# A fused attention and mixture-of-experts kernel: four more experts in the 20-product first layer, its weights built earlier, and the last expert reordered

## The chip, the cores and the metric

One core of a Trainium2 chip runs the whole program. The metric is the time of one execution on the device, in microseconds, as the median of the runs shown. The profile is of one further execution, and all rows below are from it. TensorE is called PE here, VectorE DVE, ScalarE ACT, GpSimd POOL; SP is the queue that issues nearly all DMAs.

## The reference, cut to what matters

Attention with a cluster mask makes x, and a mixture of eight experts is laid over it. B=4 batches, H=8 heads, S=768 rows, D=64, so x is 3072 x 512; each expert has w1 (512 x 1024) and w2 (1024 x 512).

```
scores = scale * q @ k.T                 # per head, 768 x 768
mask   = q_assign[:, None] == k_assign[None, :]
attn   = softmax(where(mask, scores, -1e9)) @ v
x      = attn.transpose(0, 2, 1, 3).reshape(3072, 512)
P      = exp(x @ w_gate - max), normalised 8 times by rows and by columns
for e in range(8):
    h    = maximum(x @ w1[e], 0)
    out += P[:, e:e+1] * (h @ w2[e])
```

## The kernel before

**Numbers.** Matmuls run in fp16. A fp32 value is split into a high half (a scaled fp16 copy, made on ACT) and a low half (what is left, made on DVE from the fp32 value and the high half, both in SBUF). A product of two values takes three matmuls.

**Phases.** Attention of all heads and the first batch's x take the time to about 480 us. A `Planner` orders that phase: every task (loads, splits, exponentials, reductions, outputs) has a rank from the tables `KEYS` and `NUDGES`, and `RELUCT`, `EARLY`, `PATIENCE`, `STAY`, `HOLD` and `WAIT` say when an engine's plan prefers another task. From 480 to about 897 us the first batch runs through experts 0 to 6. Then come 25 **slots**: the first batch's last expert and, for each of the second, third and fourth batch, experts 0 to 7. The program numbers batches from 0, so `(2, 4)` is the third batch's fifth expert.

**A slot.** The loop at the end of the program runs over slots. In iteration n it gives PE layer 1 of slot n and layer 2 of slot n-1, in 28 steps: a step is 9 matmuls of layer 2 (`layer2b`, 256 columns, L2303) and a piece of layer 1. All other work of the slot is a task with a step at which it is issued (`plan_slot`, `at`), and every engine runs what it gets in the order of issue.

- Layer 1 comes in two forms. `layer1b` uses 7 products of blocks in place of 8 (a Strassen form): 168 matmuls of 384 columns in a slot (L1673). `layer1c` uses 20 products in place of 24 (x in 3 x 2 blocks, w1 in 2 x 4): 240 matmuls of 256 columns (L2405). `FINE = 3` gives the second form to the fourth batch alone. DVE adds each product out of PSUM into the blocks of h (L1687), and ACT and DVE do the like for the other form.
- Layer 2 is always the 7-product form: `ORDER2` names per product the block of w2 and the block of h. `minus` (L2120, POOL, 128x768) makes the sums T1 to T4 of blocks of h, `high` (L2125, ACT) and `low` (L2129, DVE, 128x768) split the seven blocks for each half g of the hidden units: 14 lows in a slot. `evict` (L2268, L2270, DVE) scales PSUM by the gate and adds it to the output.
- The 20-product form needs combinations of x and of w1 that the other form lacks. `next_u(b)` (L1619) makes the 16 combinations of x of batch b: six loads, a maximum of each (DVE), the maximum over all partitions (`spread_powers`: a store of 128 numbers to DRAM, then the broadcast load `all<-amx`, then a DVE reduction of it), sums on POOL, a high on ACT and a low on DVE (L1649) each, and a store to `xsu`. `reload_u` loads them back before the batch. `plan_extras` (L2203) makes six combinations of w1 per expert: `load_rows`, nine POOL sums, high, low (L2196), and a store to `w1x`. All of this is done in the third batch's slots. The 7-product form of a batch has `next_x(b)` (L1583) with its own `spread_powers`.
- In the second batch's slots the w2 of later experts is also summed (POOL, L355), split (L2150 on DVE) and stored.

**The order of `inputs`.** `next_x` and `next_u` are generators that the loop advances by one yield at chosen steps: in the second batch at `INPUTS_AT = (8, 15, 22, 25)`, in the third at `UNITS_AT`, every second step from 5 on. Between the issue of the broadcast load `all<-amx` and the DVE reduction of it lie two such yields.

**The last slot.** In the iteration after the last slot only layer 2 of the fourth batch's last expert is left: 252 matmuls, with nothing beside them. `HASTE` sets the steps of a few highs and lows there.

Of the kernel before, what the change touches and what calls it, by code (L numbers as in the profile page):

```python
# [8 lines left out]
F32 = mybir.dt.float32  # L9
# [11 lines left out]
P = 128  # L21
# [37 lines left out]
class Planner:  # L59
# [127 lines left out]
def attn_moe_kernel(  # L187
# [79 lines left out]
    def powers(src, n, ps_tile, pool, use):  # L267

        yield PE, 0.13, 0.107, 0.1
        ps = ps_tile()  # L270
        nc.tensor.transpose(out=ps[0:n, 0:P], in_=src, identity=ident)
        gm = pool.tile([2, 1], F32, name="gm2")
        nc.vector.tensor_reduce(out=gm[0:n], in_=ps[0:n, 0:P], axis=AX, op=ALU.max)
        yield DVE, 0.6
# [82 lines left out]
    with ExitStack() as actx:  # L357
# [183 lines left out]
        KEYS = dict(load=-795.83, split0=-299.177, split1=-169.764, split2=-270.294, assign=-887.386, place=56.074, chain=-795.952, ones=-1730.337, max=-22.408, rows=-380.671, exp=-3.788, values=5.696, out=11.693, batch=-2279.549, store=25.266, group=419.467, vsum=-220.72, group0=-1045.745, inputs=-487.095, first=831.128, high=772.934, low=-602.628, chain1=-1478.092, ones1=1457.856)  # L541
# [925 lines left out]
    FINE = 3  # L1467
# [151 lines left out]
    def next_u(b):  # L1619
# [11 lines left out]
        for i, t in enumerate(xt):  # L1631
            largest(am6[:, i : i + 1], t)
            yield
# [453 lines left out]
    def load_unit(q):  # L2087
        n, u = loads_[q - N1]
        b, e = slots[n]
        if b < FINE:  # L2090
            return load_wa(e * NP2 + u)
# [379 lines left out]
```

## Time and profile before

| | us |
|---|---|
| runs | 2276.38, 2274.78, 2276.26 |
| median | 2276.26 |
| profiled execution | 2274.21 |
| its span in the trace | 2272.4 |

The profiled execution is 1.8 us longer than the span of its instructions; it is 2.05 us under the median. The page gives the busy time of each engine and the chain of work that ended last. The windows view gives the same by stretch of time; cut at the first layer-2 matmul of each slot, it gives a table by slot. The timeline gives single instructions and the idle time ahead of them on their engine with what ended it.

### The profile page before, as it was taken

To read this page: it belongs to the slowest core of one execution; us is meant where nothing else is said; L and a number is where in the kernel's file an instruction comes from. 1 tells how busy PE (TensorE), PEld (TensorE's weight loads), DVE (VectorE), ACT (ScalarE), POOL (GpSimd) and SP (SyncE) were. 2 spreads that over 40 slices of the span, in tenths; PEclk is the share of its full clock that TensorE was granted. 3 is DMA by queue.
4 is the path that set the end of the run, shared out by engine and by line. 5 is a ranking of instruction groups with operands and counts; after the bars stand their busy time and mean duration, and the time that the engine had idled before them with its cause. 6 is when DMAs were issued, how large, how long until landed. Compare 5 with 4: busy or idle time off the path is not lost.

```text
span 2272.4 us, 41784 instructions
## 1 busy us (share of the span) xinstructions
PE 2240.5 (99%) x16163; PEld 1591.9 (70%) x16163; DVE 1692.1 (74%) x2700; ACT 1175.6 (52%) x2125; POOL 1364.7 (60%) x1214
## 2 busy tenths in 40 slices
PE   8999999999999999999999999999999999999998
PEld 5666666645555555777777777777777788888887
DVE  7876777868677785878888877788887765556656
ACT  5676777646766763444444434444444434443432
POOL 7787878844577871666567536577776533333343
PEclk9999999999999999999999999999999999999999
DMA  7656676366767743876666556766666665555553
GB/s 155 147 146 148 166 173 161 101 217 212 247 190 222 241 142 135 289 273 205 206 233 228 199 185 229 251 214 213 214 222 227 230 196 171 160 174 164 168 167 93
DMA packets 284079, 438.35 MB, mean 193 GB/s; under 512 B 78296, under 2 KB 203048, under 8 KB 283880
## 3 DMA queue, kind: packets, MB, share of 16 engines
q1 hardware_dynamic: 283736, 435.64, 61.5%
q8 instruction: 127, 2.08, 0.4%
q14 instruction: 72, 0.59, 0.1%
q10 hardware_dynamic: 144, 0.03, 0.0%
HBM read 312.46 MB, written 94.64 MB: 179 GB/s over the span
## 4 chain that ended last, share of the span: by engine, by line
PE 93%; DVE 3%; DMA 2%; ACT 2%; issue 1%; POOL 0%; SPq 0%; DVEq 0%; ACTq 0%; POOLq 0%
PE h_ps L1673 28%; PE pb L2303 13%; PE h_ps L2405 9%; PE pa L2303 9%; PE pc L2303 8%; PE av_ps L1191 5%; PE exp_ps L1131 3%; PE o_ps L1936 3%; PE o_ps L1937 3%; PE o_ps L1938 3%; PE max_ps L1015 3%; PE exp_ps L1132 2%; PE misc_ps L740 1%; DMA kX<-ot 1%; PE misc_ps L860 1%
## 5 line engine op out<-in xcount | busy, mean ns | idle before, releaser
L2303 PEld LDWEIGHTS <-ho 128*128 128x128 f16 x6300 | 616.9, 98 | 126.1 <-DVE ho L2129 5.5
L1673 PEld LDWEIGHTS <-wa 128*128 128x128 f16 x4032 | 394.0, 98 | 235.5 <-issue 7.0
L1673 PE MATMUL h_ps<-xsT,wa 128*128 128x384 f16 x2304 | 436.0, 326 | 1.3 <-DVE u L1687 0.8
L2129 DVE TENSOR_TENSOR ho<-h,ho 128x768 f16<-128x768 f32 x300 | 363.7, 1215 | 35.4 <-ACT ho L2125 35.2
L2303 PE MATMUL pb<-w2o,ho 128*128 128x256 f16 x2700 | 342.5, 273 | 0.4 <-DVE ho L2129 0.4
L1673 PE MATMUL h_ps<-xsB,wa 128*128 128x384 f16 x1728 | 327.6, 326 | 2.2 <-DMA w2o<-w2d 2.1
L2125 ACT CAST ho<-h 128x768 f16<-128x768 f32 x300 | 240.7, 824 | 14.6 <-PE pa L2303 6.5
L2405 PE MATMUL h_ps<-xu,wa 128*128 128x256 f16 x1920 | 246.2, 273 | 0.0
L2120 POOL TENSOR_TENSOR h<-h 128x768 f32<-128x768 f32 x50 | 92.3, 1846 | 254.3 <-DVE ho L2129 239.2
L2340 ACT ACTIVATE h<-h 128x384 f32<-128x384 f32 x204 | 106.0, 519 | 254.4 <-DVE h L1687 254.2
L1019 DVE TENSOR_REDUCE mrt<-max_ps 128x1 f32<-128x512 f32 (+1 forms) x288 | 192.0, 684 | 58.1 <-PE max_ps L1015 55.5
L2303 PE MATMUL pa<-w2o,ho 128*128 128x256 f16 x1800 | 230.2, 274 | 2.2 <-DVE ho L2129 1.7
L2303 PE MATMUL pc<-w2o,ho 128*128 128x256 f16 x1800 | 228.7, 273 | 2.4 <-DVE ho L2129 2.4
L1687 DVE SCALAR_TENSOR_TENSOR u<-h_ps,m 128x384 f32<-128x384 f32 x192 | 106.0, 552 | 136.1 <-PE h_ps L1673 131.7
L2405 PEld LDWEIGHTS <-wa 128*128 128x128 f16 x1920 | 187.9, 98 | 21.7
L1153 POOL TENSOR_TENSOR psum<-psum,pe 128x512 f32<-128x512 f32 x150 | 196.7, 1324 | 9.9 <-ACT pe L1138 8.0
L1138 ACT ACTIVATE pe<-exp_ps 128x512 f32<-128x512 f32 x288 | 167.5, 598 | 52.8 <-PE exp_ps L1132 44.5
L2120 POOL TENSOR_TENSOR h<-h,T 128x768 f32<-128x768 f32 x50 | 108.0, 2160 | 138.8 <-DVE ho L2129 136.7
L1191 PE MATMUL av_ps<-pe,vn 128*64 128x512 f32 (+1 forms) x768 | 133.5, 491 | 0.0
L1938 PE MATMUL o_ps<-wb,hl 128*128 128x512 f16 x336 | 127.3, 379 | 0.0
L1937 PE MATMUL o_ps<-wb,hh 128*128 128x512 f16 x336 | 127.3, 379 | 0.0
L1936 PE MATMUL o_ps<-wb,hh 128*128 128x512 f16 x336 | 127.3, 379 | 0.0
(339 smaller groups left out, 3880.7 us busy)
## 6 DMA issues: line engine op xcount, KB each, us to landing
w2o<-w2d SPq DMA_DIRECT2D x175, 512.0 KB
wa<-w1d SPq DMA_DIRECT2D x70, 896.0 KB
r<-in_moe_w SPq DMA_DIRECT2D x60, 512.0 KB
wa<-w1d SPq DMA_DIRECT2D x224, 128.0 KB
raw<-in_moe_w SPq DMA_DIRECT2D x52, 512.0 KB
w1d<-wa SPq DMA_DIRECT2D x26, 896.0 KB
w2d<-w2s SPq DMA_DIRECT2D x28, 512.0 KB
wa<-w1x SPq DMA_DIRECT2D x48, 256.0 KB
```

The costliest lines, as they stand in the source:

```text
L1019: nc.vector.tensor_reduce(out=t["mr"][:, i0 : i0 + ni, ni - 1], in_=ps.rearrange("p (x c) -> p x c", x=ni), axis=AX, op=ALU.max)
L1153: (nc.gpsimd if e == POOL else nc.vector).tensor_tensor(out=st[:, o : o + N0], in0=old[o], in1=part, op=ALU.add)
L1191: nc.tensor.matmul(av[o, a:z], vn[:, i, :], heads[t]["pe", c][:, i - i0], start=(i == 0), stop=False, skip_group_check=True)
L1673: nc.tensor.matmul(ps[:, 0:HB], wa[:, a, w_, c, :], x[:, x_, c, :], start=(first and s_ == 0), stop=(s_ == len(steps) - 1), skip_group_che ...
L1936: nc.tensor.matmul(po[i], hh[:, t, ti], wbh[:, t], start=(first and t == 0), stop=False)
L1937: nc.tensor.matmul(po[i], hh[:, t, ti], wbl[:, t], start=False, stop=False)
L1938: nc.tensor.matmul(po[i], hl[:, t, ti], wbh[:, t], start=False, stop=(last and t == 1))
L2120: nc.gpsimd.tensor_tensor(out=t, in0=d[a], in1=d[c], op=ALU.subtract)
L2125: nc.scalar.copy(t[:, 0], blocks[n, g][o])
L2129: nc.vector.tensor_tensor(out=t[:, 1], in0=blocks[n, g][o], in1=t[:, 0], op=ALU.subtract)
L2303: nc.tensor.matmul(ps[:, q], h[:, h_, f, q * P : (q + 1) * P], w[:, 2 * g + f, w_], start=(first and g == 0 and s_ == 0 and q % 2 == 0), s ...
L2405: nc.tensor.matmul(ps[:, f], wa[:, at_ * P : (at_ + 1) * P], units[rank + x_][:, c], start=(p in FRESH and f == 0 and s_ == 0), stop=(s_ = ...
```

## The change

Five things are altered.

1. `FINE` becomes `(2, 4)` and is compared with slots: experts 4 to 7 of the third batch use `layer1c` too. `xsu` exists for both batches.
2. The combinations of w1 are made in other tasks: `load_extra`, nine sums of 128x128, one high and one low of 128x768, and a store, for each half f of each of two row blocks c, 36 sums per expert where there were 18 of 128x256. For experts 4 to 7 this lies in the second batch's slots, two slots per expert; for experts 0 to 3 in the third batch's slots 0 to 3.
3. `next_x(2)`, `next_u(3)` and `next_u(2, known=True)` (which needs no maximum) follow each other from slot (1, 1) on, at every second step from 2 on (`UNITS_AT`), in the second batch as well. `reload_u` of the third batch lies in slot (2, 3), that of the fourth inside the last 20-product layer of the third.
4. The last slot's layer 2 takes the first three products for g=0, then for g=1. `HASTE` covers more blocks, six of the split blocks go to buffers of other pools (`SPARE`), T1 of g=1 goes to a buffer of its own, and T4 is made earlier.
5. The planner's tables are new, and in the scale chain `yield DVE` stands ahead of the reduction.

```diff
-    FINE = 3
+    FINE = (2, 4)
...
-        for i, t in enumerate(xt):
-            largest(am6[:, i : i + 1], t)
-            yield
-        am = gs.tile([P, 1], F32, name="am")
-        nc.vector.tensor_reduce(out=am, in_=am6, axis=AX, op=ALU.max)
-        yield from spread_powers(am, 1, f"amx{b}", lambda g: input_use(b, g, gs))
+        if not known:
+            am6 = gs.tile([P, 6], F32, name="am6")
+            for i, t in enumerate(xt):
+                largest(am6[:, i : i + 1], t)
+                yield
...
+    def plan_extras(e, first, times):
+        for i, t in enumerate(times):
+            c, f = divmod(i, 2)
+            at(first + t[0], load_extra, e, c, f)
+            for m in range(9):
+                at(first + t[1] + m // 3, extra_sum, e, m)
+            at(first + t[1] + 3, extra_high, e)
+            at(first + t[1] + 4, extra_low, e)
+            at(first + t[1] + 7, extra_store, e, c, f)
...
-        if b == FINE - 1:
-            plan_extras(e, base - SLOT)
+        if b == 2 and e < (FINE[1] or E):
+            plan_extras(e, base - SLOT, [(5 * i - 4, 4 + 5 * i) for i in range(4)])
+        if b == 1 and FINE[1] and e >= FINE[1]:
+            n_ = slots.index((1, 2 * (e - FINE[1])))
...
+        if n == NS - 1:
+            order[0:6] = [(i, g) for g in range(2) for i in range(3)]
...
-    UNITS_AT = tuple(range(5, 27, 2))
+    UNITS_AT = tuple(range(2, 28, 2))
+    EARLY_AT = 16
...
-            if e == 1 and b + 1 < B:
-                inputs = next_u(b + 1) if b + 1 >= FINE else next_x(b + 1)
+            if e == 1 and (b + 1, 0) < FINE:
+                inputs = next_x(b + 1)
+                if b == 1 and FINE[1]:
+                    inputs = chain(inputs, next_u(3), next_u(2, True))
...
-            if s in (UNITS_AT if n < NS and slots[n][0] == FINE - 1 else INPUTS_AT):
+            if s in (UNITS_AT if n < NS and slots[n] > (1, 0) else INPUTS_AT):
```

**DVE in slot (1, 2).** A piece of DVE's queue in the iteration that has layer 1 of the second batch's third expert (1034.06 to 1088.87 us in the trace of before). `ho` are lows for layer 2, `u` and `h` from `h_ps` the adds out of PSUM, `w2s` a low of w2, `xst` a low of x. Before:

```order
L2129 TENSOR_TENSOR ho<-T_12242,ho 128x768
L2270 SCALAR_TENSOR_TENSOR acc<-pc,gates,acc 128x256 x3
L1687 SCALAR_TENSOR_TENSOR u_12381<-h_ps,m_12359 128x384
L2129 TENSOR_TENSOR ho<-h_11538,ho 128x768
L324 TENSOR_REDUCE am_11741<-xqB_11748 128x1
L2150 SCALAR_TENSOR_TENSOR w2s<-s2w,s_92,w2s 128x4x256
L1687 SCALAR_TENSOR_TENSOR u_12430<-h_ps,m_12359 128x384
L2129 TENSOR_TENSOR ho<-h_11875,ho 128x768
L1687 SCALAR_TENSOR_TENSOR h_12187<-h_ps,u_12430 128x384
L2270 SCALAR_TENSOR_TENSOR acc<-pb,gates,acc 128x256 x3
L1687 SCALAR_TENSOR_TENSOR h_12187<-h_ps,m_12359 128x384
L2129 TENSOR_TENSOR ho<-h_11537,ho 128x768
```


The same stretch with the change:

```order
L2138 TENSOR_TENSOR ho<-T_12336,ho 128x768
L2289 SCALAR_TENSOR_TENSOR acc<-pc,gates,acc 128x256 x3
L1688 SCALAR_TENSOR_TENSOR u_12485<-h_ps,m_12463 128x384
L2138 TENSOR_TENSOR ho<-h_11573,ho 128x768
L2159 SCALAR_TENSOR_TENSOR w2s<-s2w,s_92,w2s 128x4x256
L1688 SCALAR_TENSOR_TENSOR u_12535<-h_ps,m_12463 128x384
L2138 TENSOR_TENSOR ho<-h_11920,ho 128x768
L347 SCALAR_TENSOR_TENSOR xst<-xqB_11639,sx,xst 128x768
L1688 SCALAR_TENSOR_TENSOR h_12280<-h_ps,u_12535 128x384
L2289 SCALAR_TENSOR_TENSOR acc<-pb,gates,acc 128x256 x3
L1688 SCALAR_TENSOR_TENSOR h_12280<-h_ps,m_12463 128x384
L2138 TENSOR_TENSOR ho<-h_11572,ho 128x768
```


The low of x, `xst<-xqB_11639`, has come in between two lows for layer 2 and the next add; the reduction `am` of `next_x(2)` is gone from here, and those of `next_u(3)` come at the end of the iteration. Over the whole iteration six lows `xst`, two lows `w2s` of the new weights and four reductions `am` of 512 elements stand there where one reduction of 768 and one small one stood.

**SP around the broadcast load.** DMAs in the order of issue around `all<-amx`; `wa` are weights of layer 1, `w2o` of layer 2, `r` rows for the sums. Before, in slot (2, 1), for `next_u(3)`:

```order
L2133 DMA w2o<-w2d_6261 128x2048
L1562 DMA amx_17127<-am 128x1
L2133 DMA w2o<-w2d_6262 128x2048
L1580 DMA wa<-w1d_108 128x3584
L2201 DMA w1x_6299<-w2s 128x2048
L1565 DMA all_17180<-amx_17127 128x128
L2201 DMA w1x_6299<-w2s 128x1024
L2133 DMA w2o<-w2d_6262 128x2048
```


With the change there are two such places in the second batch, the first for `next_x(2)`:

```order
L1562 DMA amx_11986<-am 128x1
L2146 DMA r_12008<-in_moe_w 128x2x512
L2164 DMA w2d_6263<-w2s 128x4x512
L1565 DMA all_12038<-amx_11986 128x128
L2142 DMA w2o<-w2d_6263 128x2048
L1580 DMA wa<-w1d_108 128x3584
L2142 DMA w2o<-w2d_6263 128x2048
```


and the second for `next_u(3)`:

```order
L1562 DMA amx_13153<-am 128x1
L1580 DMA wa<-w1d_114 128x3584
L2142 DMA w2o<-w2d_6264 128x2048
L1565 DMA all_13202<-amx_13153 128x128
L2164 DMA w2d_6265<-w2s 128x4x512
L2176 DMA r_13251<-in_moe_w 128x2x256 x2
L2142 DMA w2o<-w2d_6264 128x2048
```


Between the store `amx` and the broadcast load stand two transfers in each of the two places, where three stood in the third batch.

**DVE in the last slot.** From the gates of the last expert on; `C` and `acc` are evictions. Before:

```order
L1728 TENSOR_SCALAR gates<-pr,so 128x6
L2270 SCALAR_TENSOR_TENSOR C_21954<-pb,gates,C_21954 128x256 x3
L2129 TENSOR_TENSOR ho<-h_26027,ho 128x768
L2129 TENSOR_TENSOR ho<-h_26521,ho 128x768 x2
L2129 TENSOR_TENSOR ho<-T_26586,ho 128x768
L2129 TENSOR_TENSOR ho<-T_26668,ho 128x768
L2270 SCALAR_TENSOR_TENSOR C_21954<-pa,gates,C_21954 128x256 x3
L2270 SCALAR_TENSOR_TENSOR acc<-pa,gates,acc 128x256 x6
L2270 SCALAR_TENSOR_TENSOR acc<-pc,gates,acc 128x256 x3
L2129 TENSOR_TENSOR ho<-h_26003,ho 128x768
L2129 TENSOR_TENSOR ho<-h_26067,ho 128x768
```


With the change:

```order
L1729 TENSOR_SCALAR gates<-pr,so 128x6
L2289 SCALAR_TENSOR_TENSOR C_22566<-pb,gates,C_22566 128x256 x3
L2138 TENSOR_TENSOR ho<-h_27133,ho 128x768
L2138 TENSOR_TENSOR ho<-T_27203,ho 128x768
L2138 TENSOR_TENSOR w2s<-h_26639,w2s 128x768
L2138 TENSOR_TENSOR ho<-tx,ho 128x768
L2138 TENSOR_TENSOR ho<-T_27283,ho 128x768
L2138 TENSOR_TENSOR r_27269<-h_26679,r_27269 128x768
L2138 TENSOR_TENSOR w2s<-h_27133,w2s 128x768
L2289 SCALAR_TENSOR_TENSOR C_22566<-pa,gates,C_22566 128x256 x3
L2138 TENSOR_TENSOR s2w<-h_26679,s2w 128x768
L2289 SCALAR_TENSOR_TENSOR acc<-pa,gates,acc 128x256 x6
```


The lows up to the first eviction of `pa` are seven where they were five (with `r` and `w2s` as new places of the low halves), two more, of B21 and B22, stand ahead of the gates, and the six evictions of `acc<-pa` stand behind one low more.

## Rows read from the trace of the kernel before

**Rows 1.** The page, part 1: busy us of each engine, share of the span, instructions.
```profile
PE 2240.5 (99%) x16163; PEld 1591.9 (70%) x16163; DVE 1692.1 (74%) x2700; ACT 1175.6 (52%) x2125; POOL 1364.7 (60%) x1214
```

**Rows 2.** Windows by phase: stretch and length (us), busy us (instructions), clock, DMA share, GB/s.
```profile
0.00:480.00 480.00, 461.77 (x2847) 291.17 (x2847) 360.35 (x659) 321.28 (x741) 371.98 (x450) 0.99 0.61 146
...
925.00:1830.00 905.00, 902.85 (x6961) 680.89 (x6959) 735.69 (x1088) 401.65 (x644) 565.86 (x407) 1.00 0.66 225
```

**Rows 3.** Windows by single slot, columns as in rows 2.
```profile
924.44:979.25 54.81, 54.81 (x422) 41.10 (x421) 45.67 (x66) 24.68 (x39) 38.09 (x26) 1.00 0.81 287
...
1034.06:1088.87 54.81, 54.81 (x422) 41.09 (x421) 47.25 (x66) 24.14 (x38) 37.37 (x27) 1.00 0.60 202
...
1417.73:1474.85 57.12, 54.97 (x422) 41.09 (x421) 42.77 (x78) 23.05 (x38) 32.54 (x27) 1.00 0.75 238
...
1694.09:1748.90 54.81, 54.81 (x422) 41.09 (x421) 41.49 (x65) 23.29 (x38) 33.49 (x27) 1.00 0.65 226
...
1803.39:1857.10 53.71, 53.71 (x495) 48.14 (x493) 33.89 (x54) 19.50 (x31) 19.41 (x12) 1.00 0.61 194
...
2232.41:2272.40 39.99, 30.20 (x254) 25.00 (x251) 29.23 (x44) 11.80 (x16) 12.34 (x6) 0.94 0.35 106
```

**Rows 4.** Chain of waits in a seven-product slot: start (us), us, engine, output, line, count.
```profile
1040.09 0.98 PE pa L2303 x9
1041.08 0.98 PE h_ps L1673 x6
```

**Rows 5.** Chain of waits in a twenty-product slot.
```profile
1961.73 1.31 PE h_ps L2405 x12
```

**Rows 6.** Timeline in the 57.12 us slot: start, us, instruction, [idle before <- releaser].
```profile
1463.44 0.32 SPq L1565 DMA_DIRECT2D all<-amx  x1
...
1472.06 0.29 DVE L1569 TENSOR_REDUCE gmax<-all 128x1 f32<-128x128 f32 x1 [4.64 <-DMA all<-amx]
...
1473.28 0.55 DVE L1687 SCALAR_TENSOR_TENSOR h<-h_ps,m 128x384 f32<-128x384 f32 x1
...
1473.88 1.14 PE L1673 MATMUL h_ps<-xsB,wa 128*128 128x384 f16 x6 [2.15 <-DMA w2o<-w2d]
```

**Rows 7.** Timeline of the last expert's second layer.
```profile
2235.81 1.92 PE L2303 MATMUL pc<-w2o,ho 128*128 128x256 f16 x16 [1.05 <-DVE ho L2129]
...
2241.27 1.92 PE L2303 MATMUL pc<-w2o,ho 128*128 128x256 f16 x16 [1.36 <-DVE ho L2129]
...
2250.20 5.55 PE L2303 MATMUL pa<-w2o,ho 128*128 128x256 f16 x34 [1.67 <-DVE ho L2129]
...
2263.45 4.09 PE L2303 MATMUL pb<-w2o,ho 128*128 128x256 f16 x36
...
2267.58 1.27 DVE L2270 SCALAR_TENSOR_TENSOR C<-pb,gates,C 128x256 f32<-128x256 f32 x3 [2.66 <-PE pb L2303]
```

**Rows 8.** DVE's groups by line, 924 to 1803 us: busy us, mean ns of one.
```profile
L2129 DVE TENSOR_TENSOR ho<-h,ho 128x768 f16<-128x768 f32 x193 | 251.3, 1302 | 0.0
...
L2196 DVE SCALAR_TENSOR_TENSOR w2s<-s2w,s,w2s 128x512 f16<-128x512 f32 x16 | 13.4, 840 | 0.0
...
L347 DVE SCALAR_TENSOR_TENSOR xst<-tx,sx,xst 128x768 f16<-128x768 f32 x4 | 5.0, 1248 | 0.0
...
L324 DVE TENSOR_REDUCE am<-xqB 128x1 f32<-128x512 f32 x4 | 2.7, 675 | 0.0
```

**Rows 9.** DVE's timeline in the second batch.
```profile
980.90 2.15 DVE L2129 TENSOR_TENSOR ho<-h,ho 128x768 f16<-128x768 f32 x1
...
983.45 2.37 DVE L2150 SCALAR_TENSOR_TENSOR w2s<-s2w,s,w2s 128x1024 f16<-128x1024 f32 x1
...
992.27 0.94 DVE L2129 TENSOR_TENSOR ho<-T,ho 128x768 f16<-128x768 f32 x1
```

**Rows 10.** POOL's timeline over the same time.
```profile
984.69 2.79 POOL L2120 TENSOR_TENSOR h<-h,h 128x768 f32<-128x768 f32 x1
```

**Rows 11.** POOL's groups by line, 924 to 1803 us: busy us, mean ns of one.
```profile
L2181 POOL TENSOR_TENSOR s2w<-s2w,r 128x256 f32<-128x256 f32 x96 | 95.1, 991 | 7.3
```

More of the change, by code (lines that the diff above doesn't have):

```diff
@@ L2084, in attn_moe_kernel @@
     blocks, parts_, lefts, sums_, gates_of = {}, {}, {}, {}, {}
-    loads_ = [(n, u) for n, (b, _) in enumerate(slots) for u in range(7 if b >= FINE else NP2)]
+    loads_ = [(n, u) for n in range(NS) for u in range(7 if slots[n] >= FINE else NP2)]
     def load_unit(q):
@@ L2089, in load_unit @@
         b, e = slots[n]
-        if b < FINE:
+        if slots[n] < FINE:
             return load_wa(e * NP2 + u)
@@ new lines, in extra_sum, with part @@
+        r, x = sums_[e, "r"][0], sums_[e, "x"]
+        def part(t, m):
+            return t[:, m * P : (m + 1) * P]
+        o, _, *a = EXTRAS[i]
+        old = a[0] == "x"
+        first, sign, second = a[1:] if old else a
+        quad = [part(r, int(m) % 2 * 4 + int(m) // 2) for m in (first, second)]
+        nc.gpsimd.tensor_tensor(
+            out=part(x, int(o)), in0=part(x, int(first)) if old else quad[0], in1=quad[1], op=ALU.add if sign == "+" else ALU.subtract
+        )
+        if i == 8:
+            sums_[e, "r"] = sums_[e, "r"][1:]
@@ L2216, in plan_slot @@
+    SPARE = {(o, g): x for g in range(2) for o, x in zip(("B21", "B22", "T3"), (
+        (rp, [P, 2, 2 * DO], "r2"), (sp, [P, 4, 2 * HD], "s2w"), (w2p, [P, 8, HD], "w2s"),
+    ))}
+    HASTE = {
[3 rows of a table added]
+    }
     def plan_slot(n):
@@ L2219, in plan_slot @@
         base = SLOT * (n + 1)
-        fine = b >= FINE
-        for g, (t1, t2, t3, t4) in enumerate(((-3, -2, -1, 9), (2, 3, 4, 11) if fine else (1, 2, 3, 11))):
+        fine, last = slots[n] >= FINE, n == NS - 1
+        for g, (t1, t2, t3, t4) in enumerate(((-3, -2, -1, 5 if last else 9), (1, 2, 4, 7) if last else (2, 3, 4, 11) if fine else (1, 2, 3, 11))):
             at(base + t1, minus, n, g, "T1", "B12", "B11", "B11")
@@ L2422, in attn_moe_kernel @@
     for n in range(NS + 1):
-        one = (layer1c(n) if slots[n][0] >= FINE else layer1b(n)) if n < NS else iter(())
+        one = (layer1c(n) if slots[n] >= FINE else layer1b(n)) if n < NS else iter(())
         two = layer2b(n - 1) if n else iter(())
@@ L2442, in attn_moe_kernel @@
                 f(*a)
-            if s in (UNITS_AT if n < NS and slots[n][0] == FINE - 1 else INPUTS_AT):
+            if s in (UNITS_AT if n < NS and slots[n] > (1, 0) else INPUTS_AT):
                 step(inputs)
+            if s == EARLY_AT and n + 1 < NS and slots[n + 1] == FINE:
+                for _ in inputs:
+                    pass
+                for i in (0, 1, 6, 7):
+                    reload_u(FINE[0], i)
             step(two)
```

116 lines of the change are left out of this document (54 added, 62 removed), and 3 rows, old and new, of the table HASTE.

## The prediction

> **What bounds the kernel now.** I read the page's engines first: PE is busy in 99% of the span [rows 1], so time is won only where PE's own work shrinks or where PE stands still. The windows by phase say where it stands still: 18 us of the first 480 are not busy, 2.1 of the 905 us of the second and third batch [rows 2]. Cut by slot, a slot of the second or third batch is 54.81 us long and PE is busy for all of it, a slot of the fourth batch 53.71, one slot 57.12, and the last stretch 39.99 with 30.20 of PE [rows 3]. So the slots are bound by PE's stream of matmuls, at a granted clock of 1.00; the exceptions are one stall and the tail. DVE is the next engine: 41 to 47 us of a 54.81 us slot [rows 3].
>
> The profiled execution took 2274.21 us, 2.05 under the median of 2276.26; I add the changes to the first and then 2.05.
>
> **Four slots in 20 products.** The chain of waits shows six matmuls of 384 columns in 0.98 us, so 0.163 each, and nine of 256 columns in 0.98, so 0.109 [rows 4]; in the other form twelve of 256 columns take 1.31, again 0.109 [rows 5]. Layer 1 falls from 168 x 0.1625 = 27.30 to 240 x 0.1092 = 26.20 us, so −1.10 for a slot; whole slots say the same, 54.81 − 53.71 [rows 3]. Four slots: **−4.4**. A clock or operand reason against it isn't in the rows, as the fourth batch runs this form from end to end. Its combinations of x come by DMA: one combination is used last 6 of 20 products before the next slot wants its successor, 6 x 2.7 = 16 us, against 384 KB at the 194 GB/s of such a slot [rows 3], 2 us. That is covered, at nothing; without the cover it would be 2 us for the load that comes late.
>
> **The stall in slot (2, 1).** The row of PE that stands still names a weight load, 2.15 us [rows 6]. DVE's rows tell the cause: the broadcast load `all<-amx` is issued at 1463.44, the reduction that wants it waits 4.64 us until 1472.06, and the add that PE wants stands behind it on DVE until 1473.83 [rows 6]. The transfer took 8.6 us with a DMA share of 0.75 in that slot. With the change `next_u(3)` is no longer in this slot: **−2.3** (57.12 − 54.81). But `next_x(2)` and `next_u(3)` both make such a load in the second batch now, with the reduction two yields, that is four steps of about 2 us, behind its issue, as in the slot that stalls. (`next_x(2)` had seven steps and more between.) In SP's order two transfers stand between the store and the broadcast load, where three did. Each costs between 0, where the load lands in time, and 2.15 [rows 6], together 0 to 4.3. I take **+1.5**, nearer to the lower end: 4.64 us of waiting on DVE cost 2.15 on PE, so 2.5 are hidden by the lead that DVE has, and the slots concerned, but for their neighbours, show DMA shares of 0.60 [rows 3].
>
> **DVE in the second batch.** This is the cost. New work in these slots: sums, highs, lows and stores for the weights of four experts, 16 combinations of x for each of two batches, and the maxima. In slot (1, 2) the order adds six lows of x, at 1.248 or somewhat less, 6.6 to 7.5 us; two lows of the new weights of 128x768, with 0.84 for 128x512 [rows 8], so 1.7 to 2.7; and four reductions at 0.675 [rows 8] for one of 768, +1.6. That is +10 to +11.8 on 47.25 us [rows 3]: 57.3 to 59 us of DVE in a slot of 54.81. The other seven slots, counted in the same way, get 2 to 7 us more and reach 45 to 54. Where DVE is late, PE waits for the adds, since a PSUM bank comes free only with them; up to 2.5 us late costs nothing [rows 6].
>
> The durations themselves depend on POOL. A low of 128x768 takes 0.94 alone and 2.15 where POOL runs; the low of w2 takes 2.37, and POOL's subtraction of the same time 2.79 [rows 9, 10]; the mean of all such lows is 1.30 [rows 8], with POOL busy 566 of 905 us, a share of 0.63 [rows 2]. So sharing costs 0.36 a low. POOL gets 18 sums of 128x128 more in such a slot; a sum of 128x256 takes 0.99 [rows 11], so I estimate 0.45 each and 45 us of POOL in slot (1, 2), a share of 0.82. In proportion a low grows by 0.11, and 26 lows by about 2.5 us. At the lower end, then, slot (1, 2) is 2.5 us over and the lead hides it: 0 to 0.5. At the upper it is 4.2 + 2.5 over, and two slots at 54 grow by 2 each and are over by 1 each: 9. I take **+3.5**.
>
> The Trainium skill (SBUF — State Buffer, section "Who interferes with whom") says that a DVE instruction with two inputs in SBUF and a GpSimd instruction that reads SBUF take a shared pair of ports in turn, the first for its whole instruction while the other fully blocks. The rows above agree (0.94 against 2.15). It speaks against this change, which puts such instructions on both engines in the same slots, and is the mechanism of the second rival.
>
> **The last slot.** Its layer 2 is 252 matmuls, 252 x 0.1092 = 27.5 us, yet from 2232.41 to the end of the last matmul at 2267.54 it takes 35.13 [rows 7]. PE waits for lows at three places, 1.05, 1.36 and 1.67 us [rows 7], and between them it is fed slowly. With the change two lows are made ahead of the gates, T1 of the second half gets a buffer of its own and need not wait for a low that reads the old one, and the first 108 matmuls come in the order in which halves of h are ready. Going through the new order with the durations of these rows, I find a wait of 1.2 for T2's low and one of 2.2 for the six evictions of `pa` ahead of the next product, and the last matmul 31.5 to 33 us after the first. Nothing beyond it changes (1.27 of eviction [rows 7], then the store). **−3.0**, from −4.5 to −1.5.
>
> **The attention phase.** The new ranks reorder the first 480 us; the matmuls there are the same ones. All that can be won is the 18 us in which PE is not busy [rows 2]; a third of it, 6 us, to either side is my bound, since nothing there says which tasks are late now. I take **−1.5**: the waits are many and short, which is what other ranks can move, yet they can't all go. In the third batch the moved work takes load off, but PE never waits there but for the stall, so that is worth nothing.
>
> **Sum.** −4.4 − 2.3 + 1.5 + 3.5 − 3.0 − 1.5 = −6.2: 2274.2 → 2268.0 in the profiled execution, 2270.0 as a median.
>
> **The rivals.**
> - *Same.* Both broadcast loads stall PE as the one before did (+4.3), and DVE's lateness costs 6, with the rest as above: −11.2 + 10.3 = −0.9, about 2275. For it: the same four steps, and a second batch with DMA shares to 0.81 [rows 3]. Against it: DVE's lead. The attention phase losing 6 in place of winning 1.5 ends near there too, at −6.2 + 7.5, 2277.6.
> - *Slower.* DVE becomes the bound of the second batch. If POOL's work were beside every low, sharing would cost 0.36 / 0.63 = 0.57 a low, 0.21 more than in the mean; with the longer lows of w2 that makes about 5.7 us a slot on top of the 48 to 58 us, and six slots are over 54.81, by 23 us in all. All else is −9.7, so +13: 2289.6. It decides from 14.3 us of PE's waiting on (−9.7 + 14.3 = +4.6). For it: both engines' queues are filled at the same steps. Against it: POOL has 10 us free in the fullest slot, and the adds read PSUM.
> - *Faster still.* The ranks of the attention phase are worth 6 in place of 1.5: 2265.5.
>
> **How the numbers follow.** The forecast (2270, itself 2265 to 2275) 0.56, same 0.27, slower 0.09, faster still 0.08. A measurement of this kernel tells from no change about 0.2%, 4.6 us, so 2271.7 is the line for faster: 0.45 of the forecast's 0.56 lies under it and 0.11 over it. Faster 0.45 + 0.08 = 0.53; same 0.11 + 0.27 = 0.38; slower 0.09. The range of 2263 to 2279 leaves out the slower rival and the far end of the fastest.
>
> **What would show it.** Slots (2, 4) to (2, 7) at 53.71 (right) or longer (then the loads of combinations are late); slot (2, 1) at 54.81; slot (1, 2) and its neighbours at 54.8 to 60, with PE's idle time released by DVE's adds; one row of waiting for `all<-amx` at each of two places; the last stretch at 37 in place of 39.99; PE's busy time of the first 480 us unchanged, with the layer of the first expert starting some us earlier or later. If slots of the second batch other than (1, 2) are over 56, the term of DVE is wrong; if the last stretch is over 39, that of the tail.

## The result

The changed kernel takes 2303.6 us (median of 4 runs, 2302.66 to 2307.62) against 2276.32 before: a ratio of 1.0124, interval 1.0106 to 1.0141 (ratios here and below are those on record; that of the two medians is 1.0120). It is 27 us slower where 6 us less were forecast. The profiled execution took 2303.82 us with a span of 2302.0.

The page's first part, as rows 1 before:

```profile
PE 2244.9 (98%) x16451; PEld 1618.3 (70%) x16451; DVE 1704.1 (74%) x2685; ACT 1194.3 (52%) x2141; POOL 1453.8 (63%) x1381
```

PE's busy time is 4 us more than in [rows 1], though four slots have less to compute, and POOL has 89 us more. The windows by slot, each cut at the slot's first layer-2 matmul (stretch and length, then busy us of PE, PEld, DVE, ACT and POOL with their instructions, granted clock, DMA share, GB/s), answer to [rows 3]:

```profile
921.19:976.00 54.81, 54.81 (x422) 41.09 (x420) 48.13 (x68) 26.36 (x41) 50.26 (x44) 1.00 0.85 300
976.00:1043.21 67.21, 58.56 (x423) 42.44 (x421) 54.84 (x78) 26.73 (x41) 48.48 (x45) 0.95 0.69 233
1043.21:1107.23 64.02, 56.40 (x421) 41.01 (x420) 59.63 (x75) 30.62 (x46) 50.30 (x44) 1.00 0.82 285
1107.23:1168.50 61.27, 56.69 (x423) 41.64 (x421) 50.40 (x80) 27.44 (x43) 45.81 (x45) 0.97 0.81 232
...
1224.24:1283.46 59.22, 56.64 (x421) 41.84 (x420) 53.70 (x74) 29.07 (x46) 52.03 (x47) 0.97 0.76 259
...
1338.68:1393.49 54.81, 54.81 (x422) 41.10 (x420) 44.13 (x66) 24.02 (x40) 35.32 (x32) 1.00 0.70 232
1393.49:1450.46 56.97, 55.13 (x422) 41.08 (x420) 47.50 (x71) 26.49 (x43) 46.82 (x49) 1.00 0.79 264
1450.46:1505.82 55.36, 55.11 (x423) 41.09 (x421) 46.37 (x70) 26.41 (x43) 44.53 (x48) 1.00 0.71 233
...
1616.34:1670.05 53.71, 53.71 (x495) 48.14 (x492) 31.36 (x51) 19.49 (x32) 19.43 (x12) 1.00 0.59 181
...
2260.20:2302.00 41.80, 30.57 (x254) 25.59 (x251) 30.08 (x42) 9.39 (x13) 14.95 (x7) 0.90 0.33 101
```

The second batch's slots, 54.81 us each before, are 54.81, 67.21, 64.02, 61.27, 55.74, 59.22, 55.22 and 54.81: 33.8 us more. The first slot starts 3.3 us earlier than before. The 20-product slots are at 53.71, as forecast. The third batch's first three slots are 56.97, 55.36 and 56.03, the last stretch 41.80 in place of 39.99 (41.76 and 39.95 if it is counted from the start of its first matmul itself, as below). So −3.3 + 33.8 + 1.3 (third batch, experts 0 to 3) − 4.1 (experts 4 to 7) + 1.8 (last stretch) are 29.5, and the span is 29.6 longer.

What PE waited for, over the whole span (engine, line, releaser: us in total, times, longest):

```profile
PE h_ps L1674 <- DVE h L1688: 16.6, 13, 3.6
PE h_ps L1674 <- DVE u L1688: 10.3, 8, 4.1
...
PE pb L2324 <- DVE ho L2138: 3.5, 1, 3.5
...
PE pa L2324 <- DVE acc L2289: 2.3, 1, 2.3
```

The first two groups are the adds out of PSUM on DVE. In the second batch alone they are 16.0 and 7.9 us, and no other wait of PE is listed there. The whole second batch in one window, before and with the change:

```profile
924.44:1362.92 438.48, 438.48 (x3362) 328.77 (x3361) 363.62 (x523) 195.49 (x308) 264.97 (x180) 1.00 0.66 225
...
921.19:1393.49 472.30, 448.02 (x3362) 331.27 (x3360) 414.10 (x572) 221.79 (x344) 386.35 (x339) 0.99 0.77 255
```

So the 33.8 us have two parts: for 24.3 PE is not busy, and 9.5 are PE's own busy time, 448.0 in place of 438.5 for the same matmuls. Most of the second part (7.5) lies in the three slots with a granted clock of 0.95 to 0.97. DVE is busy for 414 of the 472 us, and the mean of its lows, here from 921 to 1616 us, has hardly moved from [rows 8]:

```profile
L2138 DVE TENSOR_TENSOR ho<-h,ho 128x768 f16<-128x768 f32 x145 | 192.4, 1327 | 0.9 <-ACT ho L2134 0.8
```

So DVE is not out of time there; it stands still. What it waits for in the second batch, besides PE:

```profile
DVE gmax L1569 <- DMA all<-amx: 9.5, 2, 5.7
DVE am L324 <- DMA xqB<-xd: 7.1, 2, 3.6
DVE w2s L2207 <- ACT w2s L2203: 7.0, 5, 2.6
```

and what ACT waits for on POOL in the second batch (before, the second of these groups had 10.0 us in 8 waits, and the first didn't exist):

```profile
ACT w2s L2203 <- POOL s2w L2190: 36.8, 12, 7.3
...
ACT w2s L2155 <- POOL s2w L355: 12.1, 10, 2.6
```

Two thirds of POOL's new sums of 128x128, from 921 to 1616 us (the others take 0.72 in the mean):

```profile
L2190 POOL TENSOR_TENSOR s2w<-s2w,r 128x128 f32<-128x128 f32 x192 | 125.3, 653 | 15.0
```

Two patterns make up these waits. The first is a read that stands too close behind its DMA. In slot (1, 1), for `next_x(2)`:

```profile
1027.83 0.33 SPq L1565 DMA_DIRECT2D all<-amx  x1
...
1031.36 1.15 PE L2324 MATMUL pb<-w2o,ho 128*128 128x256 f16 x9
...
1033.65 0.28 DVE L1569 TENSOR_REDUCE gmax<-all 128x1 f32<-128x128 f32 x1 [5.70 <-DMA all<-amx]
...
1036.04 0.55 DVE L1688 SCALAR_TENSOR_TENSOR u<-h_ps,m 128x384 f32<-128x384 f32 x1
...
1036.64 1.14 PE L1674 MATMUL h_ps<-xsT,wa 128*128 128x384 f16 x6 [4.14 <-DVE u L1688]
...
1037.62 1.95 PE L2324 MATMUL pb<-w2o,ho 128*128 128x256 f16 x9
```

The broadcast load is issued at 1027.83; its reduction waits 5.70 us at the head of DVE's queue, the add behind it ends at 1036.6, and PE has stood still for 4.14. The nine matmuls of layer 2 after the gap take 1.95 us, the nine ahead of it 1.15: PE runs at a lower granted clock there (0.80 from 1036 to 1039, 0.63 from 1039 to 1042). The second pattern is in the chain of waits at the end of slot (1, 4) (start, us, engine, output):

```profile
1218.69 0.42 POOL s2w L2190
...
1220.19 0.94 ACT w2s L2203
...
1221.16 1.58 DVE w2s L2207
...
1223.21 2.02 DVE ho L2138
1225.24 2.21 DVE xst L1650
1227.44 0.48 DVE h L1688
...
1227.97 1.17 PE h_ps L1674 x6
```

POOL's last sum of a piece of the new weights ends at 1220.2; ACT's high of it waits at the head of ACT's queue, DVE's low for the high, and behind that low stand another low, a low of x and then the add that PE needs: four engines in a row, each in order.

### The profile page after: what moved, and what is told of

The parts are those of the page before. It is cut to its first block, busy times and chain, and to the rows that moved or that the text cites. A ratio compares the mean times of both kernels' runs of the same rounds, so it can differ in the third digit from the quotient of the medians.

```text
span 2302.0 us, 42812 instructions
## 1 busy us (share of the span) xinstructions
PE 2244.9 (98%) x16451; PEld 1618.3 (70%) x16451; DVE 1704.1 (74%) x2685; ACT 1194.3 (52%) x2141; POOL 1453.8 (63%) x1381
## 4 chain that ended last, share of the span: by engine, by line
PE 76%; DVE 11%; POOL 5%; DMA 4%; issue 2%; ACT 2%; SPq 0%; DVEq 0%; POOLq 0%; ACTq 0%
PE h_ps L1674 15%; PE h_ps L2429 14%; PE pb L2324 9%; PE pc L2324 6%; PE pa L2324 6%; PE av_ps L1191 5%; PE exp_ps L1131 3%; PE max_ps L1015 3%; PE exp_ps L1132 3%; PE o_ps L1937 2%; PE o_ps L1938 2%; PE o_ps L1939 2%; DVE ho L2138 2%; POOL s2w L2190 2%; POOL s2w L355 2%
## 5 line engine op out<-in xcount | busy, mean ns | idle before, releaser
L1674 PEld LDWEIGHTS <-wa 128*128 128x128 f16 x3360 | 329.3, 98 | 236.7 <-issue 41.0
L1674 PE MATMUL h_ps<-xsT,wa 128*128 128x384 f16 x1920 | 364.2, 327 | 22.8 <-DVE h L1688 11.7
L2429 PE MATMUL h_ps<-xu,wa 128*128 128x256 f16 x2880 | 369.3, 273 | 0.0
L2429 PEld LDWEIGHTS <-wa 128*128 128x128 f16 x2880 | 281.8, 98 | 32.6
L1674 PE MATMUL h_ps<-xsB,wa 128*128 128x384 f16 x1440 | 275.8, 328 | 7.6 <-DVE h L1688 4.9
L2361 ACT ACTIVATE h<-h 128x384 f32<-128x384 f32 x156 | 81.0, 520 | 175.7 <-DVE h L1688 175.3
L1688 DVE SCALAR_TENSOR_TENSOR u<-h_ps,m 128x384 f32<-128x384 f32 x160 | 88.1, 551 | 100.1 <-PE h_ps L1674 93.7
L2406 ACT ACTIVATE h<-h_ps 128x512 f32<-128x512 f32 x108 | 64.4, 596 | 171.3 <-PE h_ps L2429 125.2
L2396 POOL TENSOR_TENSOR h<-h,tx 128x512 f32<-128x512 f32 x12 | 23.0, 1913 | 204.2 <-DVE tx L2408 204.2
L2190 POOL TENSOR_TENSOR s2w<-s2w,r 128x128 f32<-128x128 f32 x192 | 125.3, 653 | 15.0
L2408 DVE SCALAR_TENSOR_TENSOR h<-h_ps,h 128x512 f32<-128x512 f32 x96 | 65.2, 689 | 92.4 <-PE h_ps L2429 73.8
```

The source lines that it names most:

```text
L1674: nc.tensor.matmul(ps[:, 0:HB], wa[:, a, w_, c, :], x[:, x_, c, :], start=(first and s_ == 0), stop=(s_ == len(steps) - 1), skip_group_che ...
L1688: nc.vector.scalar_tensor_tensor(out=t, in0=ps[:, 0:HB], scalar=KAPPA, in1=x, op0=ALU.mult, op1=ALU.add)
L2190: nc.gpsimd.tensor_tensor(out=part(x, int(o)), in0=part(x, int(first)) if old else quad[0], in1=quad[1], op=ALU.add if sign == "+" else AL ...
L2429: nc.tensor.matmul(ps[:, f], wa[:, at_ * P : (at_ + 1) * P], units[rank + x_][:, c], start=(p in FRESH and f == 0 and s_ == 0), stop=(s_ = ...
```

## The experiments

The theories: (1) data are read too soon behind their DMA; (2) DVE has too much work, shared with POOL; (3) POOL is behind its steps, and ACT and DVE wait for it in order. The table gives by how many us the second batch's slots (1, 1) to (1, 6) exceed 54.81. The slots are those of one profiled execution each, and so is the time, but for the first row. Two runs further down (old form of the last expert, T1 in place) have the same second batch as the changed kernel, and theirs exceeds by 35.9 and 32.4 us in all where the changed kernel's does by 33.8, so 2 us more or less in such a sum are noise.

| kernel | (1,1) | (1,2) | (1,3) | (1,4) | (1,5) | (1,6) | time |
|---|---|---|---|---|---|---|---|
| changed | 12.4 | 9.2 | 6.5 | 0.9 | 4.4 | 0.4 | 2303.6 |
| later reads | 2.1 | 12.6 | 0 | 5.6 | 4.4 | 0.5 | 2298.3 |
| no four weights | 3.3 | 7.1 | 3.5 | 0.2 | 0.5 | 1.5 | 2285.7 |
| wide sums | 6.3 | 9.8 | 6.4 | 0 | 1.1 | 1.5 | 2290.5 |
| later reads, wide sums | 0 | 5.5 | 0.9 | 2.1 | 1.1 | 1.7 | 2277.6 |
| later reads, no four weights | 0 | 1.6 | 0 | 0.3 | 0.5 | 1.5 | 2273.7 |
| fourth batch only | 3.5 | 7.2 | 0 | 0 | 0 | 0 | 2297.5 |
| the same, old steps | 0 | 0 | 0 | 0 | 0 | 0 | 2280.4 |

The kernel before took 2276.2 us beside later reads, no four weights and fourth batch only, 2275.7 beside wide sums and old steps, and 2273.5 beside the two combined edits.

**Later reads** (first run).

```diff
+            for _ in range(2):      # behind the loads of x
+                yield
...
+        for _ in range(more):       # 2, behind the broadcast load
+            yield
```

> The changed kernel, but in the second batch's slots four yields more lie between a DMA and the DVE instruction that reads what it brought: two (about 8 us) between the loads of x and the first maximum, two more between the broadcast load and its reduction, for both inputs. Theory 1 (DVE, which works in order, stands still for data that was asked for too late, and PE with it): the four DVE waits of 3.5, 5.7, 3.6 and 3.8 us go, PE's gaps of 3.3, 4.1 and 3.6 us in slots (1,1) to (1,3) with them; 2303.6 falls by 9 to 14 us to about 2292. Theory 2 (DVE has simply more work than time in these slots, shared with POOL): the waits only let DVE catch up less; under 4 us are won, at least 2299.5.

2298.3: 5.3 us, between the two; the second batch is 8.5 shorter and the third 2.9 longer. DVE's waits for DMAs are gone and with them most of the excess of (1, 1) and all of that of (1, 3), but the work that moved on made (1, 2) and (1, 4) longer. There ACT waits 4.7 and 7.9 us for POOL's sums, and 5.8 and 6.6 for a store of the new weights, for which it waited 2.0 in the second batch of the changed kernel:

```profile
ACT w2s L2161 <- DMA w1x<-w2s: 14.0, 3, 6.6
```

The names suggest that the high of w2 wants a buffer `w2s` that this store still reads; no run tests that. Theory 1 is right for two slots and is not the whole.

**No weights for the four experts** (second run).

```diff
-                nc.sync.dma_start(out=o, in_=w1x[e][:, :, EXTRA.index(p)])
+                nc.sync.dma_start(out=o, in_=w1x[e % FINE[1]][:, :, EXTRA.index(p)])
...
-            plan_extras(e, SLOT * n_, [...])
```

> The changed kernel without the new weights of experts 4 to 7: their sums, highs, lows, loads and stores in the second batch's slots are left out, and the 20-product layer of these experts reads the combinations of expert e-4 (same sizes and times). Theory 2 (too much work on DVE and POOL): PE is held up by 33.8 us in the second batch; the 16 lows and 144 sums are the larger part of what is new, so 14 to 22 us are won, about 2285. Theory 1 (reads too soon behind their DMAs): the four waits stay, slots (1,1) to (1,3) stay over 58 us, and less than 8 us are won, over 2295.

2285.7, 18 us less. (1, 1) to (1, 3) still exceed by 14, as theory 1 says. The weights' work is the larger part of the loss; the run takes away its load on DVE and POOL, its lateness and its transfers together, so it doesn't tell them apart.

**The fourth batch only, and the old steps** (third and sixth run).

```diff
-    FINE = (2, 4)
+    FINE = (3, 0)
```

> The changed kernel with the 20-product first layer in the fourth batch alone: no weights and no combinations of x for it in the second batch. All else is as changed (ranks of the attention phase, last expert, weights in pieces of 128 columns). If the second batch's work is the whole loss: the second batch's slots are at 54.81 again; 2276.3 - 3.2 (attention, earlier start of the first slot) + 1.8 (last slot) gives 2273 to 2277. If the smaller pieces of the weights or their short runs in the stores cost by themselves, the third batch's slots are above 55.5 and the time is over 2280.

2297.5, far over what was expected, and not for the reason that was named: (1, 1) and (1, 2) exceed by 3.5 and 7.2 as with the four experts, since `next_x(2)` keeps its close steps; the third batch's slot (2, 1) is 62.4 (57.12 before), again at the broadcast load. The last stretch was 43.3 here. Next, the steps as before on top of it:

```diff
-    UNITS_AT = tuple(range(2, 28, 2))
+    UNITS_AT = tuple(range(5, 27, 2))
...
-            if s in (UNITS_AT if n < NS and slots[n] > (1, 0) else INPUTS_AT):
+            if s in (UNITS_AT if n < NS and slots[n][0] == 2 else INPUTS_AT):
```

> The kernel of the third run (20 products in the fourth batch alone) with the steps for the inputs as before the change: four per slot in the second batch, every second step from 5 on in the third. If the closer steps of next_x(2) alone held up slots (1,1) and (1,2) there (58.3 and 62.0 us): both are at 54.81 again, and the time falls by at least 10.6 us, to 2284 to 2287; the third batch's slots stay above 54.81 where the new weights are made in smaller pieces. If the order of the attention phase or the form of the weights did it, they stay over 57 and the time over 2292.

All eight slots of the second batch are at 54.81 again, and the time is 2280.4, under the range expected, with an earlier start and a shorter third batch than in the run above. So the close steps alone cost 10.6 us in the second batch, with none of the new work there. The third batch's slots stay at 55.6 to 58.6 (54.81 at (2, 6)), as expected with the weights in smaller pieces: that batch takes 450.4 us where it took 440.5 before.

**Wide sums** (fifth run). Three POOL sums of 256 columns in place of nine of 128:

```diff
-            for m in range(9):
-                at(first + t[1] + m // 3, extra_sum, e, m)
+            for m in range(3):
+                at(first + t[1] + m, wide_sum, e, m)
```

> The changed kernel with three POOL sums of 256 columns in place of nine of 128 for each piece of the new weights; the sums are not those that the weights need. DVE's and ACT's instructions and all DMAs stay. Theory 3 (POOL is behind its steps with the nine sums; ACT's high waits for them, in order, DVE's low waits for the high, in order, and PE for the add behind that low): ACT's waits for these sums in the second batch fall from 36.8 us to under 10, the excess of slots (1,3) to (1,6) from 12.2 us to under 4, and the time by 8 to 14 us to 2290 to 2296. Theory 2 (DVE's own load of lows and adds is too much): DVE has the same load, under 4 us are won, at least 2299.

2290.5, 13.1 us less, with DVE's instructions untouched; ACT's waits for these sums fall to 13.9 us, not under 10. That is theory 3's range, though (1, 3) stays at 6.4, held by the broadcast load. 8.8 us come from the second batch, the rest from the third and an earlier start. DVE is busy for as long as before the edit:

```profile
919.17:1382.65 463.48, 444.74 (x3362) 329.85 (x3360) 413.89 (x572) 221.96 (x344) 337.36 (x243) 0.99 0.78 261
```

So the gain doesn't come from a shorter time of DVE's work, which speaks against the reading that POOL cost these 8.8 us by slowing DVE's lows.

**Both edits, and later reads without the weights** (ninth and tenth run). The edits are those of the first with the fifth, and of the first with the second.

> The changed kernel with both earlier edits: the four yields of the first run and the three wide sums of the fifth (sums that the weights don't need). If early reads and POOL's lateness are separate causes, their gains add, 5.3 + 13.1: about 2285, with the waits of DVE for loads gone and ACT's waits for the sums under 15 us. If the two stand in for one another (what one gives up the other takes): 2289 or more.

> The changed kernel without the new weights of experts 4 to 7 (the layer reads those of expert e-4) and with the four yields. Of the 16.1 us by which the second batch's slots were too long without the weights, slots (1,1) and (1,3) gave 6.8 and slot (1,2), which has the lows of x, 7.1. If early reads explain the first and DVE's load the second: (1,1) and (1,3) near 54.81, the slot with the lows of x still 59 to 63, about 2279. If early reads explain all: 2272. If the close steps load DVE throughout: 2284.

2277.6, below both numbers expected, and 2273.7, between the first two, with the slot of the lows of x at 56.4, under its range. In the second batch the later reads save 8.5 us, the wide sums 8.8, both 22.6. That they gain more together fits a lead that each cause uses up for the other, and gaps that cost more by the clock when they are long; no run separates these two. With both, ACT's waits for the new sums are nearly gone, and DVE's work is still all there:

```profile
ACT w2s L2218 <- POOL s2w L2207: 4.6, 3, 2.2
...
918.49:1368.17 449.68, 441.19 (x3363) 328.63 (x3361) 410.79 (x568) 219.48 (x341) 336.96 (x240) 1.00 0.80 266
```

DVE is busy for 410.8 us, against 414.1 in the changed kernel and 363.6 before, and the excess is 11.2 us in place of 33.8: the amount of work on DVE is not what cost the other 22.6.

With the reads later and no weights the fullest slot is 1.6 over:

```profile
1028.43:1084.85 56.42, 55.16 (x423) 41.06 (x421) 54.89 (x78) 29.84 (x45) 39.25 (x27) 1.00 0.78 277
```

DVE is busy 54.89 of 56.42 us there, and the second batch exceeds by 3.8 in all: without the weights' work the share of theory 2 is small. What the 11.2 us with both edits are made of stays open: ACT waits 8.5 us there for stores of the new weights. A run with the highs and lows of the weights at later steps, the straight test of theory 3, was not made.

**The attention phase** (seventh run), and the stall of slot (2, 1) (eighth run, with `more` = 2 as in the first), on the kernel before:

```diff
-        KEYS = dict(load=-795.83, ...)      # and the other tables, as in the change
+        KEYS = dict(load=-362.213, ...)
```

> The kernel before with only the new ranks and planner's constants of the attention phase and the place of the yield in the scale chain. The first slot starts 3.2 us earlier, as in the changed kernel, and nothing gives it back: 2272.5 to 2273.5. If the later phases use up the lead (the first batch's slots are paced by loads): 2275 to 2277.

2269.6 against 2275.7: 0.9978, interval 0.9968 to 0.9988, so 2.7 to 7.3 us. The sign was right; the size is open, since the phase itself varies: with the same ranks the first slot started at 918.1 us in this profile and at 925.0 in the next one.

> The kernel of the run beside it with two yields (about 8 us) more between the broadcast load of next_u and its reduction. If DVE's wait for that load is the whole of the 57.12 us slot: it is 54.81 us long and the time 2.3 us less than beside it, 2270 to 2271. If another load is late there, under 1 us.

Slot (2, 1) is 54.81 in place of 57.34 us: the broadcast load was the whole of that stall. The time is 2268.9 (0.9971, 0.9962 to 0.9980), 0.6 from the run beside it, which these runs don't resolve.

**The last expert.** The old form in the changed kernel (fourth run; order, `HASTE`, `SPARE`, T1 and T4 as before the change):

> The changed kernel with the order, buffers and steps of the last expert as before. If the new order of the last expert is worse by itself (two pairs of lows beside POOL's subtractions at 2.55 us each): the stretch from its first matmul to the end falls from 41.8 to 40.0 us, and the time by about 1.8 to 2301.8. If something ahead of it made it longer, it stays at 41 to 42.

2303.0; the last stretch is 38.33 in place of 41.76 us, so the new form is worse by itself. (The same old form took 39.95 in the kernel before, where the granted clock was 0.59 and 0.56 from 2250 to 2254 us; here it stayed at 1.00.) In the changed kernel:

```profile
2266.17 2.55 DVE L2138 TENSOR_TENSOR ho<-T,ho 128x768 f16<-128x768 f32 x1
2267.87 2.52 POOL L2124 TENSOR_TENSOR h<-h,h 128x768 f32<-128x768 f32 x1
...
2268.65 2.55 DVE L2138 TENSOR_TENSOR w2s<-h,w2s 128x768 f16<-128x768 f32 x1
...
2268.78 3.60 PE L2324 MATMUL pb<-w2o,ho 128*128 128x256 f16 x16 [3.50 <-DVE ho L2138]
...
2278.69 2.43 DVE L2289 SCALAR_TENSOR_TENSOR acc<-pa,gates,acc 128x256 f32<-128x256 f32 x6
...
2281.18 4.09 PE L2324 MATMUL pa<-w2o,r 128*128 128x256 f16 x36 [2.33 <-DVE acc L2289]
```

Three lows in a row (two are shown) take 2.55 or 2.56 us each, one beside each subtraction on POOL (2.52); PE waits 3.50 for the first, then 2.33 for evictions that stand behind the lows on DVE. Four runs looked for the cause, the first in the changed kernel, the others with the new form of the last expert in the kernel of the eighth run; the edits, in their order:

```diff
# T1 in place
-        if n == NS - 1 and (o, g) == ("T1", 1):
-            t = tmp.tile([P, KC, HB], F32, name="tx")
# evictions first
-        ("T3", 0): (2, 2), ... ("B21", 1): (1, 6), ("T3", 1): (7, 7), ("B22", 1): (2, 8),
+        ("T3", 0): (2, 9), ... ("B21", 1): (1, 10), ("T3", 1): (7, 11), ("B22", 1): (2, 12),
# old order
-        if n == NS - 1:
-            order[0:6] = [(i, g) for g in range(2) for i in range(3)]
# on DVE
-        nc.gpsimd.tensor_tensor(out=t, in0=d[a], in1=d[c], op=ALU.subtract)
+        (nc.vector if n == NS - 1 else nc.gpsimd).tensor_tensor(out=t, in0=d[a], in1=d[c], op=ALU.subtract)
```

> The changed kernel with T1 of the last expert's second half in its old place, so that POOL waits there again for the low that reads the block. If the wait that was taken away had kept POOL from running beside DVE's lows (2.55 us each in the changed kernel, 0.94 alone): POOL pauses, the two lows there take under 2 us, PE's wait of 3.5 us ahead of the third product falls under 2, its clock stays at 1.00, and the last stretch falls from 41.8 to about 39.5. If the order of the products is at fault: it stays at 41.5 to 43.

44.97: the first wait falls to 1.36, as said, but lows still take 2.40 to 2.56, only later, and the evictions come later still (a wait of 6.25). Theory fallen.

> The kernel of the eighth run (the kernel before with the new ranks and a later read of the broadcast load) with the new order and buffers of the last expert, but with the four lows that the first six products don't need (T3 of both halves, B21 and B22 of the second) moved behind the nine evictions of pa on DVE. If DVE's queue is what held up the new tail (lows ahead of the lows and evictions that PE waits for): the last stretch takes 37 to 39.5 us (41.8 in the changed kernel, 39.95 with the old order), without a wait for acc<-pa over 1 us, and the time is 2267 to 2269. If the order of the products or POOL's subtractions hold it up: 41 or more, and 2270 to 2272.

In this kernel the low of B21's second half reads a block that T4 has overwritten, so that part of the output is another; the amount of work is the same. 41.29, not the 37 to 39.5 expected: no wait of PE for an eviction over 1 us is left, the first wait is still 3.49. The evictions are not the cause of that one.

> The kernel of the eighth run with all that the change does to the last expert (buffers, steps of highs, lows and T4) but for the order of the products: product for product, with both halves of h, as before. If the new order is at fault because it asks for T2 of the first half after 36 matmuls, where the old one asks after 72: PE's wait of 3.5 us ahead of that product falls under 1 us, the clock stays at 1.00 there, and the last stretch takes under 39.5 us, against 39.95 with everything of it old and 41.3 to 41.8 with everything of it new. If the lows are slow because POOL works beside them whatever the order, the wait moves to another product and the stretch takes 40.5 us or more.

42.43: the wait moves to the next product (5.29), as the second reading said. The order is not the cause.

> The kernel of the eighth run with the whole new form of the last expert (order, buffers, steps), but with that expert's eight subtractions on DVE in place of POOL. If the lows are slow because DVE and POOL take turns (one low for each subtraction, 2.5 us each): lows and subtractions take 0.94 each on DVE, the first wait of 3.5 us falls under 1.5, and the last stretch takes 38 to 40.5 us against 41.3 to 41.8. If DVE's amount of work in the tail is what counts: it has 7.5 us more, and the stretch takes over 42.

42.01, at the edge of the second reading, and the signs of both are there: the turns are gone and the first wait is 1.11, but with the subtractions on DVE too the evictions come late and PE waits 5.20 for them (timeline):

```profile
2231.22 0.95 DVE L2139 TENSOR_TENSOR ho<-T,ho 128x768 f16<-128x768 f32 x1
...
2232.22 1.92 PE L2322 MATMUL pb<-w2o,ho 128*128 128x256 f16 x16 [1.11 <-DVE ho L2139]
...
2245.42 6.09 PE L2322 MATMUL pa<-w2o,r 128*128 128x256 f16 x36 [5.20 <-DVE acc L2287]
```

> The kernel of the eighth run (old form of the last expert) with that expert's eight subtractions on DVE. In the old form POOL's and DVE's work alternate with pauses, so little is to be had by taking turns away: if so, the last stretch takes 38.5 to 40.5 us against 39.95 (or 38.3 without the low clock). If DVE's amount of work counts: over 42.

The old form with the subtractions on DVE takes 36.69 us, below the range expected, and all lows there take 0.94 to 0.96:

```profile
2234.68 0.95 DVE L2131 TENSOR_TENSOR ho<-h,ho 128x768 f16<-128x768 f32 x1
...
2243.86 3.88 PE L2305 MATMUL pa<-w2o,ho 128*128 128x256 f16 x34 [1.67 <-DVE ho L2131]
```

So the new form fails by two things: its additional early lows take turns with POOL, and they stand ahead of the evictions on DVE. Taking away one alone lets the other decide; a run of the new form without both was not made. The kernel with the old form, the subtractions on DVE, the new ranks and the later read has the lowest time of all: 2267.98 us against 2276.76 (0.9959, 0.9944 to 0.9974). Its last stretch is shorter by 3.3 than in the eighth run, but in the whole time the two are not told apart, since their intervals overlap.

## Why the prediction was wrong

- *Four slots in 20 products*: right. 53.71 each, −4.1 where −4.4 was said (the last of the four had been 54.49, not 54.81); the reloads cost nothing.
- *The stall in slot (2, 1)*: the cause was read rightly, and the run with the later read shows it. But the slot came to 55.36: DVE waits 1.9 us there for a high of the third batch's new weights. "Worth nothing" was wrong for the third batch: its first three slots are 2.2, 0.6 and 1.2 over 54.81.
- *The two broadcast loads*: sized wrong. They were bounded at 2.15 each, by the one stall before; PE's gaps behind them were 4.14 and 3.61. The DMA share was read as 0.60 from a whole slot; while DVE waited for the first load, from 1030 to 1036 us, it was 1.04 and 1.02. Two more reads of that kind weren't seen at all: the maxima that stand one yield behind the loads of x (3.5 and 3.6 us of DVE). The closer steps were read for the broadcast load alone, where every read behind a load in `next_x` and `next_u` moved closer. DVE waited 16.6 us for DMAs in all in the second batch.
- *DVE in the second batch*: this is the term that failed, 33.8 us with the reads where 3.5 + 1.5 were taken and 9 + 4.3 were the ends. Its sums of DVE's work held: slot (1, 2) has 59.6 us (57.3 to 59 forecast), and the others 44 to 55 (45 to 54). The step that failed is "up to 2.5 us late costs nothing", used as if each slot began with that lead and DVE were late by its sum alone. A queue in order is late by each wait at its head, too: the lows of the new weights waited for ACT, and ACT 36.8 us for POOL. POOL's 18 sums in a slot were costed as something that lengthens lows; that they come late and hold two other queues was not among the rivals. They were also taken too short, 0.45 us each, where they took 0.65 and 0.72 in the mean, and POOL was busy for 50.3 us of slot (1, 2) in place of 45. The lower clock behind PE's gaps, most of the 9.5 us by which PE's own busy time grew, stood nowhere in the sum, which counts each wait at its length. The sign that the prediction itself gave for a wrong term came: slots (1, 1), (1, 3) and (1, 5) are over 56. (26 lows by 0.11 are 2.9 and not 2.5; nothing hangs on it.)
- *The slower rival* had the sign and named the second batch, but by another mechanism, lows that grow longer beside POOL by 5.7 us a slot. The mean low is 1.33 us against 1.30, and the wide sums, which halve the time of POOL's new sums (98.7 to 46.4 us), gained 13 us with DVE as busy as before, 413.9 us against 414.1. The page of the Trainium skill that was cited (SBUF — State Buffer, "Who interferes with whom") agrees with the last expert's rows, where lows come one for each subtraction and take 0.95 us with POOL idle; in the second batch the turns were not what decided.
- *The last expert*: −3.0 forecast, +1.8 measured, over the 39 that was named as the sign of a wrong term. The waits of 1.2 and 2.2 us were at the places named, and the second one was sized right (2.33). The first was 3.50, since the lows were walked through at durations of the old order, where POOL pauses; and the low clock behind it was not counted.
- *The attention phase*: −1.5 taken; between −2.7 and −7.3 on the kernel before.

## What to carry to other kernels

Before work is added to an engine with spare time, look not only at its sum but at what stands at the head of its queue: each new instruction that waits for a DMA or for another engine delays everything behind it, and the waits pass on from queue to queue. Steps at which data are read need the distance to their DMA that the trace shows, here 5.3 to 8.6 us from the issue of a load to the reading of it. Two such causes hide each other: in the second batch each edit alone gained some 8.5 us, and both together 22.6.

## What the runs showed of the hardware

A gap of PE can cost more than its length. Windows of the last stretch in the changed kernel, columns as above:

```profile
2264.00:2266.00 2.00, 0.68 (x5) 0.21 (x3) 2.00 (x4) 1.97 (x3) 1.92 (x2) 1.00 0.00 0
...
2268.00:2270.00 2.00, 1.22 (x6) 0.89 (x7) 2.00 (x2) 0.77 (x1) 2.00 (x1) 0.50 0.00 0
2270.00:2272.00 2.00, 2.00 (x12) 1.40 (x10) 2.00 (x2) 0.83 (x1) 2.00 (x2) 0.50 0.00 0
...
2274.00:2276.00 2.00, 2.00 (x21) 1.80 (x19) 2.00 (x3) 0.00 (x0) 0.41 (x1) 1.00 0.14 23
```

PE stands still from 2265.28 to 2268.78, and then the granted clock is 0.50 (the 1.2 GHz level) to 2272 and over: 18 matmuls of 256 columns take 2.74 us in place of 2.13. The same followed the gaps of 3.3, 4.1 and 3.6 us in slots (1, 1) and (1, 3) and one of 2.58 in slot (1, 5); after the one of 2.15 us [rows 6] the clock stayed at 1.00. The slots' clocks of 0.95 to 0.97 above are these stretches. The length of the gap alone doesn't tell which it will be: in the last stretch before the change a wait of 1.67 us [rows 7] was followed by 0.59 and 0.56, with PE busy for 0.38 of the 2 us ahead, and the same wait in the fourth run by 1.00, with PE busy for 0.42 of 2 us there too.
